# Attention beside a feed-forward gate on one core: the flags of the single-element waits taken one turn later, and the second score pair issued one row later

## The chip, the cores and the metric

The kernel runs on one core of a Trainium2 chip, in one launch. The metric is the device time of that launch in microseconds (us). Three runs of the kernel before took 1266.8, 1267.47 and 1267.58 us, a median of 1267.47.

## What is computed

```
xn = layernorm(x)                                   # x: 2048 x 512, float32
q, k, v = split(xn @ wqkv)                          # 32 heads of 16
p = softmax(q @ k^T * 16**-0.5)                     # 32 x 2048 x 2048
s = (p @ v) @ wo
h = relu(xn @ w1 + b1); g = silu((h * h) @ w2 + b2) # 512 -> 1792 -> 512
return x + s * g
```

## The kernel before

Everything is float32. Matrix products other than scores and values split their operands into a high and a low part (`fp32r`) and add three products; the scores do the same inside one contraction of 64 rows. The order of the instructions on each engine is written out by hand; nothing is scheduled afterwards, and semaphores are set from what each instruction reads and writes.

A first stage normalises x, makes q, k and v and writes q and k to memory. Then comes the main loop, 128 turns of four steps. A step `i` is one block of 128 keys against one block of 512 queries for a group of four heads, taken as two pairs `p` of two heads. Four turns finish one block of queries; the results of the values then leave `acc`.

The scores land in PSUM. Two buffers `S` of two banks alternate. `scores(i, p)` (L282) writes a whole pair into the next of them: two matmuls, one on the upper and one on the lower 64 rows of the array, side by side. `exps(i, p, src)` (L286) is ScalarE's exponential of a pair, into an SBUF tile `P`. Of the four steps of a turn one (`i + 3`) goes another way: `aside` (L300 to L305) computes one score at a time into the lone bank `single` (the profile's `lin`), VectorE copies it to `P` (L305), and the exponential works in place.

Between the scores TensorE works off the feed-forward products: `lin(...)` issues one half-array matmul of the current pair of blocks on the upper half, the lower, or both (L330; the bank pair is `spare`). `lin(0, 1)` is one row: two matmuls side by side. At the end of a turn come its values (L561, 32 matmuls into `acc`), then `finish`, which after every fourth turn copies `acc` out, on VectorE (L100) or, in turns with `turn_ends_first`, on ScalarE (L98).

`scores(i + 1, 0)` and `scores(i + 1, 1)` at the head of a turn reuse the buffers whose exponentials were the last two of the turn before. Between them stands `see` (L780 to L786), which touches single elements, so that an engine waits for another once and later instructions need no wait of their own for it:

- on ScalarE (L784), a copy of one element that the last exponential wrote, if `act_waits`;
- on VectorE (L786), the maximum of one element of the last exponential and one of the score buffer that it read, if `dve_waits`. As it reads that buffer, the next writer of the buffer, `scores(i + 1, 1)`, waits for it instead of ScalarE.

Where a flag is off, later instructions carry the wait themselves: the second pair waits for ScalarE directly, and the bank copy (L305) and the exponentials each get a second wait.

The flags are a list `alone` of two, computed in each turn `n`. Both are off in the turns of `tanh_in` (26, 28, 54, 56, 82, 84, 110, 112), in which ScalarE also does a tanh late in the turn. The first is off in turns with `turn_ends_first` (7, 15, 23 of each 28 up to 107). The second is off in every fourth turn (`n % 4 == 3`) without `turn_ends_first`. The second also decides about one more VectorE copy late in the same turn (L840).

```python
        alone = [n not in tanh_in and not turn_ends_first[0],
                 n not in tanh_in and (n % 4 < 3 or turn_ends_first[0])]
        if n:
            see(i, last[1], *alone)
```

Of the kernel before, what the change touches and what calls it, by code (L numbers as in the profile page):

```python
# [73 lines left out]
def fast_path(tc, sb, ps, env):  # L74
# [11 lines left out]
    def t(shape, dt, tag):  # L86

        cnt[0] += 1
        p = ps if tag in ("S", "lin", "acc") else sb
        if tag in BUFS:  # L90
            turn[tag] = turn.get(tag, -1) + 1
            n = turn[tag] % BUFS[tag]
            tag = f"{tag}{places[n] if tag == 'S' else n}"
        return p.tile(shape, dt, tag=tag, name=f"{tag}_{cnt[0]}")
# [183 lines left out]
    def score(i, p, hp, dst):  # L278
        qd, qc, kb = steps[i]
        k, q = ka[qd, kb // 8], qa[qd, qc]  # L280
        r = slice(64 * hp, 64 * hp + 64)
        mm(dst, k[r, p, 128 * (kb % 8):128 * (kb % 8) + 128], q[r, p], start=True, stop=True)  # L282

    def exps(i, p, src):
        if src is not None:
            act.activation(ptile[i, p], src, AF.Exp, scale=SCALE)  # L286

    def place(i, p):
        ptile[i, p] = t([128, 2, 512], FT, f"P{2 * ((i - 1) % 4) + p}")

    def scores(i, p):

        if i < len(steps):
            sc = t([128, 2, 512], FT, "S")
            place(i, p)
            for hp in range(2):
                score(i, p, hp, sc[:, hp])
            return sc

    def aside(i, p, hp):  # L300

        if hp == 0:
            place(i, p)
        score(i, p, hp, single)
        dve.tensor_copy(ptile[i, p][:, hp], single)  # L305
# [51 lines left out]
    def lin(*halves):  # L357
        if pair[0]:
            for half in halves:
                j = half ^ swapped[0]  # L360
                pair[0][j].issue(half, lin_banks[j])

    def lin_part(half, part):
        if pair[0]:
            j = half ^ swapped[0]
            pair[0][j].issue_part(half, lin_banks[j], part)

    def swap():
        if pair[0]:
            while any([pair[0][half ^ swapped[0]].issue(half, lin_banks[half ^ swapped[0]]) for half in range(2)]):  # L370
                pass
            swapped[0] ^= 1
            if not swapped[0]:
                pair[0][0].evict()
                pair[0] = None
# [21 lines left out]
    def split_piece(eng=None):  # L397
        if at_piece[1] == len(pieces):
            return
        j, layer, m = pieces[at_piece[1]]  # L400
        at_piece[1] += 1
        raw, q = raws.pop(0), PAIRS[m][1]
        wf[layer, m] = [t([128, 4, 256] if layer == 1 else [128, 2, 512], FR, f"wf{layer}{p}{q}") for p in "hl"]
        split(*wf[layer, m], raw, eng or dve, pool)
        load_piece()
# [149 lines left out]
    def values(i):  # L555
        qd, qc, kb = steps[i]
        if kb == 0:
            acc[0] = t([128, 512], FT, "acc")
        for j in (1, 2, 3, 0) if i % 2 else (0, 1, 2, 3):
            o = (4 * qd + j) * 17  # L560
            mm(acc[0][32 * j:32 * j + 32], vt[:, kb, o:o + 32], ptile[i, j // 2][:, j % 2],  # L561
               start=kb == 0, stop=kb == NK - 1)

    def finish(i):

        qd, qc, kb = steps[i]
        if kb < NK - 1:
            return
        if i == len(steps) - 1:
            return  # L570
        ou = t([128, 512], FT, "ou")
        cast(act if turn_ends_first[0] else dve, ou, acc[0])
        sp.dma_start(zdram[qd][qc], ou[16::32])
        for j in range(4):
            sp.dma_start(udram[qd // 2][qc][0, qd % 2, :, j], ou[32 * j:32 * j + 16])
        n = i // 4
        events.setdefault(2 * n + 2, []).insert(0, (load_sums, (qd, qc)))
        at(n + 2, rowsums, qd, qc)
# [24 lines left out]
    def gate_start(c, i):  # L603
        assert (c, i) in complete
        e = t([128, 2, 512], FT, "T")
        act.activation(e, y[c, i], AF.Tanh, scale=0.5)
        gated[c, i] = e
# [101 lines left out]
    tanh_in = {}  # L709
# [44 lines left out]
    def happen(time):  # L754
        for fn, a in events.pop(int(2 * time), ()):
            fn(*a)


    n = turn["S"]
# [7 lines left out]
    def rest(i, dst):  # L767

        group(dst, lambda p: onorm[2, 3][p][:, cut[i]], lambda p: wos[0][p][:, 3])

    def end_rest(i, src):

        o = t([128, 512], FT, f"wf2{'hl'[i // 2]}{i % 2}")
        dve.scalar_tensor_tensor(o, src, 0.5, gsb[2, i // 2][:, i % 2], op0=OP.mult, op1=OP.mult)
        pool.dma_start(out[1024 + 128 * i:1152 + 128 * i], o, accum_op=OP.add)

    turn_ends_first = [False]
    seen = t([1, 16], FT, "seen")

    def see(i, other, act_waits, dve_waits):  # L780

        last = ptile[i, 1][:1, 1, 511:]
        if act_waits:
            act.copy(seen[:, :1], last)  # L784
        if dve_waits:
            dve.tensor_tensor(seen[:, 8:9], last, other[:1, 0, :1], op=OP.max)  # L786

    for n in range(TURNS):
        i = 4 * n
        happen(n)  # L790
        make, end, split_now = fill[n]
        turn_ends_first[0] = n < LAST and end and not make and fill[n - 1][2] and n % per in (7, 15, 23)

        alone = [n not in tanh_in and not turn_ends_first[0],
                 n not in tanh_in and (n % 4 < 3 or turn_ends_first[0])]
        if make:
            pair[0] = make()
        pair0 = scores(i + 1, 0)
        if n:
            see(i, last[1], *alone)  # L800
        exps(i + 1, 0, pair0)
        aside(i + 3, 0, 0)
        lin(1)
        exps(i + 1, 1, scores(i + 1, 1))
        for _ in range(3):
            lin(0, 1)
        lin(0)
        if make and end:
            lin(1)
            lin(0)  # L810
            aside(i + 3, 0, 1)
        else:

            lin_part(1, 0)
            aside(i + 3, 0, 1)
            lin(0)
        exps(i + 2, 0, scores(i + 2, 0))
        if make and end:
            for j in range(2):
                pair[0][j].issue_whole(lin_banks[j])  # L820
            swap()
        else:
            lin_part(1, 1)
            lin(0, 1)
            lin(0, 1)
        exps(i + 2, 1, scores(i + 2, 1))
        aside(i + 3, 1, 0)
        lin(1)
        exps(i + 3, 0, ptile[i + 3, 0])
        if n in tanh_in:  # L830
            gate_start(*tanh_in[n])
        lin(0, 1)
        lin(0, 1)
        last = [scores(i + 4, 0)]
        lin(0, 1)
        lin(0, 1)
        lin(0)
        aside(i + 3, 1, 1)
        if alone[1]:
            dve.tensor_copy(seen[:, 8:9], single[:1, :1])  # L840
        exps(i + 3, 1, ptile[i + 3, 1])
        last.append(scores(i + 4, 1))
        for p in range(2):
            exps(i + 4, p, last[p])
        if n == TURNS - 1:
            two = t([128, 2, 512], FT, "S")
            rest(0, two[:, 0])
        swap()
        if n == LAST - 1:
            gsb.update({(2, i): y[2, i] for i in range(2)})  # L850
        if n == TURNS - 1:
            end_rest(0, two[:, 0])
        happen(n + 0.5)
        if split_now:
            split_piece()
        for j in range(4):
            values(i + j)
        finish(i + 3)
# [169 lines left out]
```

## Time and profile before

| what | value |
|---|---|
| median of three runs | 1267.47 us |
| the profiled execution, its own time | 1267.24 us |
| its span, first to last instruction | 1265.4 us |
| granted TensorE clock over the span | 0.998 |
| TensorE matmuls busy (PE) | 1246.9 us |
| ScalarE busy (ACT) | 1056.0 us |
| VectorE busy (DVE) | 693.3 us |
| single-element maximum on DVE (L786) | 99 times, 143 ns median |
| single-element copy on ACT (L784) | 107 times, 190 ns median |

The profile is that of one execution. A row of the timeline gives start and duration in us, engine, line, operation, output and inputs by the program's names, shapes and a count; a bracket at its end says how long the engine sat idle before and what ended that. PE's busy time is that of pipelined matmuls, whose ends are modelled. A group of two matmuls that run side by side on the halves of the array appears as one row with x2, and a row cut by the window that was asked for shows a smaller count.

### The profile page before, as it was taken

What the parts mean: (1) busy time and instruction counts of PE and PEld (TensorE: products, weight loads), DVE (VectorE), ACT (ScalarE), POOL (GpSimd) and SP (SyncE); (2) the same over time, 40 slices, a digit from 0 to 9 for tenths busy, and PEclk for the clock granted to TensorE, in tenths of its full rate; (3) what the DMA queues carried; (4) which work ended last, traced back from release to release, by engine and by line L of the source; (5) the groups of instructions that cost most, each with busy time, mean ns of one, the idle gap of its engine ahead of it and who ended that gap; (6) DMA issues with size and microseconds to landing.
All of it is one profiled execution on the core that took longest, in us unless ns stands there. A gap on an engine that the chain in (4) does not pass through costs nothing.

```text
span 1265.4 us, 24423 instructions
## 1 busy us (share of the span) xinstructions
PE 1246.9 (99%) x10029; PEld 715.3 (57%) x10029; DVE 693.3 (55%) x1263; ACT 1056.0 (83%) x1230; POOL 258.9 (20%) x150
## 2 busy tenths in 40 slices
PE   8999999999999999999999999999999999999997
PEld 7888755555555455555555555555555555554554
DVE  5542255555565664545465555555554646566655
ACT  4222599999999899999998999999999999998994
POOL 5000122122211221312022221120331212222112
PEclk9999999999999999999999999999999999999999
DMA  7565513231233232131423222333222132464445
GB/s 265 209 233 190 222 46 103 59 93 54 82 127 110 60 107 61 42 91 48 153 74 110 60 76 60 93 126 107 61 63 89 45 91 56 143 217 126 139 133 119
DMA packets 84937, 137.28 MB, mean 108 GB/s; under 512 B 26059, under 2 KB 40409, under 8 KB 83285
## 3 DMA queue, kind: packets, MB, share of 16 engines
q1 hardware_dynamic: 81668, 126.25, 31.4%
q0 software_dynamic: 2720, 8.65, 2.5%
q8 instruction: 79, 1.29, 0.4%
q10 hardware_dynamic: 432, 0.79, 0.2%
q14 instruction: 38, 0.30, 0.1%
HBM read 94.24 MB, written 41.41 MB: 107 GB/s over the span
## 4 chain that ended last, share of the span: by engine, by line
PE 91%; DVE 4%; issue 2%; ACT 1%; POOL 1%; DMA 0%; DVEq 0%; ACTq 0%
PE acc L561 32%; PE spare L330 25%; PE S L282 16%; PE S L111 9%; PE lin L282 6%; ACT P L286 1%; PE spare L350 1%; DVE T L413 1%; DVE P L305 1%; PE S L204 1%; DVE T L414 0%; DVE T L677 0%; PE spare L339 0%; POOL hl L104 0%; DVE ou L100 0%
## 5 line engine op out<-in xcount | busy, mean ns | idle before, releaser
L286 ACT ACTIVATE P<-S 128x1024 f32<-128x1024 f32 x768 | 735.7, 1018 | 55.4 <-PE S L282 54.4
L305 DVE COPY P<-lin 128x512 f32<-128x512 f32 x512 | 353.7, 691 | 363.2 <-PE lin L282 321.8
L561 PE MATMUL acc<-P,vt 128*32 128x512 f32 x4096 | 466.0, 595 | 0.0
L282 PE MATMUL S<-QA,KA 64*128 64x512 f32 x1536 | 340.0, 418 | 5.5 <-DVE seen L786 5.1
L286 ACT ACTIVATE P<-P 128x1024 f32<-128x1024 f32 x256 | 270.7, 1058 | 26.6 <-DVE P L305 16.8
L561 PEld LDWEIGHTS acc<-P,vt 128*32 128x32 f32 x4096 | 120.8, 109 | 266.0 <-issue 264.5
L282 PEld LDWEIGHTS S<-QA,KA 64*128 64x128 f32 x1536 | 152.7, 183 | 181.7 <-ACT P L286 123.3
L282 PE MATMUL lin<-QA,KA 64*128 64x512 f32 x512 | 206.1, 402 | 0.7 <-DVE P L305 0.5
L104 POOL TENSOR_TENSOR wf1l<-wr,wf1h 128x1024 fp32r<-128x1024 f32 x28 | 66.8, 2386 | 404.4 <-DVE wf1h L100 137.1
L104 POOL TENSOR_TENSOR hl<-T,hh 128x1024 fp32r<-128x1024 f32 x28 | 67.6, 2414 | 237.5 <-PE S L282 151.3
L104 POOL TENSOR_TENSOR wf2l<-wr,wf2h 128x1024 fp32r<-128x1024 f32 x28 | 66.7, 2382 | 206.2 <-PE acc L561 140.5
L282 PEld LDWEIGHTS lin<-QA,KA 64*128 64x128 f32 x512 | 94.2, 184 | 20.3 <-DVE P L305 6.3
L330 PE MATMUL spare<-xl,wf1h 64*128 64x512 f32 x440 | 105.5, 391 | 0.0
L330 PE MATMUL spare<-xh,wf1h 64*128 64x512 f32 x504 | 95.7, 390 | 0.0
L330 PE MATMUL spare<-xh,wf1l 64*128 64x512 f32 x504 | 95.6, 391 | 0.0
L330 PE MATMUL spare<-wf2l,hh 64*128 64x512 f32 x400 | 94.9, 391 | 0.0
L330 PE MATMUL spare<-wf2h,hh 64*128 64x512 f32 x448 | 85.7, 390 | 0.0
L330 PE MATMUL spare<-wf2h,hl 64*128 64x512 f32 x416 | 80.8, 390 | 0.0
L98 ACT CAST P<-S 128x512 fp32r<-128x512 f32 x30 | 17.7, 588 | 57.6 <-PE S L111 55.8
L330 PEld LDWEIGHTS spare<-xh,wf1h 64*128 64x128 f32 x504 | 59.8, 185 | 8.5
L330 PEld LDWEIGHTS spare<-xh,wf1l 64*128 64x128 f32 x504 | 60.1, 185 | 7.1
L330 PEld LDWEIGHTS spare<-xl,wf1h 64*128 64x128 f32 x440 | 60.0, 184 | 1.3
(213 smaller groups left out, 1150.5 us busy)
## 6 DMA issues: line engine op xcount, KB each, us to landing
wr<-in_B_w_dram SPq DMA_DIRECT2D x56, 512.0 KB
KA<-kd SPq DMA_DIRECT2D x64, 256.0 KB
QA<-qd SPq DMA_DIRECT2D x128, 128.0 KB
kd<-P SPq DMA_DIRECT2D x15, 512.0 KB
qd<-P SPq DMA_DIRECT2D x15, 512.0 KB
u<-ud SPq DMA_DIRECT2D x15, 512.0 KB
P<-in_A_x_dram SPq DMA_DIRECT2D x8, 512.0 KB
xd<-KA SPq DMA_DIRECT2D x4, 1024.0 KB
```

Of the source, the lines that this page charges most:

```text
L98: act.copy(dst, src)
L104: leng.tensor_tensor(lo, src, hi.bitcast(FT), op=OP.subtract)
L111: mm(dst, lhs(a, k), rhs(b, k), start=n == 0, stop=n == len(todo) - 1)
L204: nc.tensor.transpose(pt[:, k, 128 * j:128 * j + 128], xnorm[c, i][:, j, 128 * k:128 * k + 128], ident)
L282: mm(dst, k[r, p, 128 * (kb % 8):128 * (kb % 8) + 128], q[r, p], start=True, stop=True)
L286: act.activation(ptile[i, p], src, AF.Exp, scale=SCALE)
L305: dve.tensor_copy(ptile[i, p][:, hp], single)
L330: mm(bank, self.lhs(a, k)[r], self.rhs(b, k)[r], start=n == 0 and self.at[other] == 0, stop=n == len(self.todo[half]) - 1 and self.at[othe ...
L350: mm(bank[:, c], self.lhs(a, k)[r], self.rhs(b, k)[r, c], start=False, stop=False)
L413: dve.tensor_scalar(r[:, f], spare[:, f], b1t[:, 2 * m + f:2 * m + f + 1], 0.0, op0=OP.add, op1=OP.max)
L561: mm(acc[0][32 * j:32 * j + 32], vt[:, kb, o:o + 32], ptile[i, j // 2][:, j % 2], start=kb == 0, stop=kb == NK - 1)
```

## The change

`see` in turn `n` gets the flags that were computed in turn `n - 1`. In turn 1 they are those of turn 0. The flag of the late copy (L840) stays that of its own turn. Second, one of the three rows `lin(0, 1)` that stood behind the second score pair now stands ahead of it.

```diff
+    alone = []
     for n in range(TURNS):
...
-        alone = [n not in tanh_in and not turn_ends_first[0],
-                 n not in tanh_in and (n % 4 < 3 or turn_ends_first[0])]
+        alone, now = [n not in tanh_in and not turn_ends_first[0],
+                      n not in tanh_in and (n % 4 < 3 or turn_ends_first[0])], alone
         if make:
             pair[0] = make()
         pair0 = scores(i + 1, 0)
         if n:
-            see(i, last[1], *alone)
+            see(i, last[1], *now)
         exps(i + 1, 0, pair0)
         aside(i + 3, 0, 0)
         lin(1)
+        lin(0, 1)
         exps(i + 1, 1, scores(i + 1, 1))
-        for _ in range(3):
+        for _ in range(2):
             lin(0, 1)
         lin(0)
```

The built program has 100 maxima on VectorE instead of 99 and 107 copies on ScalarE as before. The maximum is left out in turns 4, 12, 20, 32, 40, 48, 60, 68, 76, 88, 96, 104, 116, 120, 124 and 29, 57, 85, 113, where it was, and is there in turns 3, 11, 19, 31, 39, 47, 59, 67, 75, 87, 95, 103, 115, 119, 123, 127 and 26, 54, 82, 110, where it was not. ScalarE's copy is left out in the turns behind `turn_ends_first` (8, 16, 24 and so on) and behind a tanh (27, 29 and so on), and is there in the turns themselves.

## The prediction

> **What bounds the kernel now.** I read the page's head and its chain first, then the main loop as one window, the waits, and at last single turns in the timeline.
>
> ```profile
> span 1265.4 us, 24423 instructions
> ...
> PE 1246.9 (99%) x10029; PEld 715.3 (57%) x10029; DVE 693.3 (55%) x1263; ACT 1056.0 (83%) x1230; POOL 258.9 (20%) x150
> ...
> PE 91%; DVE 4%; issue 2%; ACT 1%; POOL 1%; DMA 0%; DVEq 0%; ACTq 0%
> ```
> ```profile
> 155.10:1244.90 1089.80, 1083.82 (x9212) 584.47 (x9210) 616.15 (x1094) 1003.29 (x1145) 233.82 (x115) 1.00 0.30 92
> ```
> ```profile
> PEld S L282 <- DVE seen L786: 20.3, 46, 1.1
> ```
> The chain is TensorE almost throughout, and the window (127 turns, from the first values block to the last; its columns are us, busy time of PE, PEld, DVE, ACT, POOL, then clock and DMA) shows a clock of 1.00. So the matmul stream sets the time, and the change, which adds no matmul and drops none, can only move TensorE's stalls. The waits name one that fits: 46 times the weight load of a score pair sat until the single-element maximum at L786. Its 20.3 us overstate the loss, since a matmul was still running for part of each wait. How much is lost shows in the pitch of the turns: a turn is the time from one values block (`acc`, L561) to the next. I number turns from 0, as the loop does. First the head of turn 13, an undisturbed one:
>
> ```profile
> 258.52 0.64 PE L561 MATMUL acc<-P,vt 128*32 128x512 f32 x4
> ...
> 262.09 0.50 PE L282 MATMUL S<-QA,KA 64*128 64x512 f32 x2
> 262.43 0.39 PE L282 MATMUL lin<-QA,KA 64*128 64x512 f32 x1
> 262.63 1.03 ACT L286 ACTIVATE P<-S 128x1024 f32<-128x1024 f32 x1 [0.38 <-PE S L282]
> 262.67 0.39 PE L282 MATMUL S<-QA,KA 64*128 64x512 f32 x2
> 262.86 0.69 DVE L305 COPY P<-lin 128x512 f32<-128x512 f32 x1 [0.65 <-PE lin L282]
> 262.90 1.09 PE L330 MATMUL spare<-xh,wf1h 64*128 64x512 f32 x7
> 263.56 1.02 ACT L286 ACTIVATE P<-S 128x1024 f32<-128x1024 f32 x1
> ...
> 266.94 0.64 PE L561 MATMUL acc<-P,vt 128*32 128x512 f32 x4
> ```
> It takes 266.94 - 258.52 = 8.42 us. Two half-array matmuls run side by side, so a "row" costs the step from one start to the next: 262.90 - 262.67 = 0.23 us. The first score pair starts at 262.09 and the second at 262.67, 4.15 after the values block began. Turn 12 stands before it:
>
> ```profile
> 249.63 0.64 PE L561 MATMUL acc<-P,vt 128*32 128x512 f32 x4
> ...
> 253.35 0.69 DVE L100 COPY ou<-acc 128x512 f32<-128x512 f32 x1 [2.01 <-PE acc L561]
> 253.96 0.13 DVE L786 TENSOR_TENSOR seen<-P,S 1x1 f32<-1x1 f32 x1
> 254.15 0.50 PE L282 MATMUL S<-QA,KA 64*128 64x512 f32 x2 [0.20 <-DVE seen L786]
> ```
> Every fourth turn a result block ends, and DVE copies `acc` out. The maximum queues behind that copy and ends at 254.09. The second pair waits for it and starts at 254.15, 4.52 after the values block began and so 0.37 later than in turn 13; the turn takes 258.52 - 249.63 = 8.89 us, 0.47 more. That is the stall at issue.
>
> All 127 turns at 8.42 would be 1069.3 us; eight turns with a denser fill (4 and 5 of each 28) have more matmul time of their own, so the whole recoverable excess is below 1089.8 - 1069.3 = 20.5 us. That is a ceiling.
>
> **The change part by part.** From the two lists of flags as the code computes them, the maximum on DVE disappears in 19 turns (4, 12, 20, 29 and so on) and appears in 20 (3, 11, 19, 26 and so on). ACT's copy disappears in 20 and appears in 20. A single-element operation is 0.14 us on DVE and hides there; what matters is who waits.
>
> *A: 15 turns lose the maximum right behind DVE's `acc` copy* (4, 12, 20 of each 28, and 116, 120, 124). The second pair then waits for ACT's last exponential only, which was done before the pair started. What remains is shown by turn 28, which has DVE's `acc` copy and no maximum already now:
>
> ```profile
> 386.03 0.64 PE L561 MATMUL acc<-P,vt 128*32 128x512 f32 x4
> ...
> 389.75 0.69 DVE L100 COPY ou<-acc 128x512 f32<-128x512 f32 x1 [1.99 <-PE acc L561]
> 389.94 0.39 PE L282 MATMUL lin<-QA,KA 64*128 64x512 f32 x1
> ...
> 390.44 0.69 DVE L305 COPY P<-lin 128x512 f32<-128x512 f32 x1
> 391.22 0.46 PE L282 MATMUL lin<-QA,KA 64*128 64x512 f32 x1
> ...
> 394.52 0.64 PE L561 MATMUL acc<-P,vt 128*32 128x512 f32 x4
> ```
> It takes 394.52 - 386.03 = 8.49 us, 0.07 over the undisturbed turn: the copy of the lone score bank (L305) is late, and with it the next use of that bank. So a turn of kind A goes from 8.89 to 8.49: 0.40 saved, 15 x 0.40 = 6.0. The stall goes to the next `lin` matmul, which is late by those 0.07. At the end of the kernel DVE is later still:
>
> ```profile
> 1143.80 0.67 DVE L100 COPY ou<-acc 128x512 f32<-128x512 f32 x1
> 1144.45 0.67 DVE L305 COPY P<-lin 128x512 f32<-128x512 f32 x1
> 1144.58 0.50 PE L282 MATMUL S<-QA,KA 64*128 64x512 f32 x2 [0.60 <-DVE seen L786]
> 1145.72 0.40 PE L282 MATMUL lin<-QA,KA 64*128 64x512 f32 x1
> ```
> This is turn 116. Its bank copy can start when the `acc` copy ends, at 1144.47, and ends by 1145.16; in turn 28 `lin` followed such a copy by 391.22 - 391.13 = 0.09, so here it comes near 1145.25 where it now comes at 1145.72. That is 0.47; I keep 0.40. Bounds for A: 0.13 a turn (only the maximum's own duration, if the copy behind it was the real holder) and 0.47 (everything): 2.0 to 7.1.
>
> *B: 20 turns gain the maximum.* They lack it today and pay turn 28's 0.07; with it they look like turn 13. 20 x 0.07 = 1.4. Below, 0; above, the same 1.4.
>
> The bank copy starts 390.44 - 389.94 = 0.50 after `lin` in turn 28 and 262.86 - 262.43 = 0.43 in turn 13: the 0.07 again.
>
> By the Trainium skill (Perfetto Trace Analysis, section Identifying Dependency Chains) an instruction that waits for several engines may get separate semaphore instructions ahead of it; the bank copy without a maximum is such a one, and the trace agrees with its 0.07. By that rule alone A would cost 15 x 0.07 = 1.05 and not save 6.0, and the sum would give 1262.6. Turn 28 holds this cost already, so the sum stays with the rows.
>
> *C: turns behind a tanh on ACT lose both waits* (27, 29 and so on, 8 in all).
>
> ```profile
> 377.45 0.64 PE L561 MATMUL acc<-P,vt 128*32 128x512 f32 x4
> ...
> 398.69 0.14 DVE L786 TENSOR_TENSOR seen<-P,S 1x1 f32<-1x1 f32 x1 [0.24 <-ACT P L286]
> ...
> 403.27 0.64 PE L561 MATMUL acc<-P,vt 128*32 128x512 f32 x4
> ```
> Turn 27 takes 386.03 - 377.45 = 8.58, turn 29 takes 403.27 - 394.52 = 8.75. In turn 29 the maximum itself waits for ACT, and the second pair behind it for both; waiting for ACT alone, one row later, it has what it needs in time. Both fall to 8.49: 4 x 0.09 + 4 x 0.26 = 1.4. Bounds: 0 and 4 x 0.16 + 4 x 0.33 = 2.0, with no rest at all.
>
> *D: the row ahead of the second pair.* The same matmuls run in another order, so where nothing waits it costs nothing on TensorE, and where the second pair waits it covers 0.23 us. The cover of its cost on ACT: the second exponential starts at 263.56, behind the first; its scores now end at 262.67 + 0.39 = 263.06, and at 263.29 one row later. ACT follows its scores by 0.04 (262.59 to 262.63), so 263.56 - 263.33 = 0.23 us of margin are left. Turns that keep a late maximum gain the full row: turn 118, for one.
>
> ```profile
> 1157.35 0.64 PE L561 MATMUL acc<-P,vt 128*32 128x512 f32 x4
> ...
> 1161.57 0.13 DVE L786 TENSOR_TENSOR seen<-P,S 1x1 f32<-1x1 f32 x1
> ...
> 1166.15 0.64 PE L561 MATMUL acc<-P,vt 128*32 128x512 f32 x4
> ```
> 8.80 us, 0.38 lost, 0.23 of it covered; five such turns (108, 114, 118, 122, 126): 1.15. Five first-layer turns lose a little, as turn 14 does (next fence: 275.45 - 266.94 = 8.51): 5 x 0.08 = 0.4. Bounds: 0 and 5 x 0.38 + 0.4 = 2.3.
>
> *E: turns in which ACT makes the `acc` copy.* Twelve of them lose ACT's copy behind it, the twelve before get one.
>
> ```profile
> 215.75 0.64 PE L561 MATMUL acc<-P,vt 128*32 128x512 f32 x4
> ...
> 219.95 0.18 ACT L784 COPY seen<-P 1x1 f32<-1x1 f32 x1
> 220.04 1.01 ACT L286 ACTIVATE P<-S 128x1024 f32<-128x1024 f32 x1
> ...
> 224.30 0.64 PE L561 MATMUL acc<-P,vt 128*32 128x512 f32 x4
> ...
> 275.45 0.64 PE L561 MATMUL acc<-P,vt 128*32 128x512 f32 x4
> 283.91 0.64 PE L561 MATMUL acc<-P,vt 128*32 128x512 f32 x4
> ```
> Turn 8 takes 8.55, 0.13 over, with ACT late. Without its copy the exponentials start 220.04 - 219.95 = 0.09 earlier; I take 0.07 for 11 turns (108 is in D): 0.8. Turn 15, one of those before, takes 283.91 - 275.45 = 8.46 and should reach 8.42: 12 x 0.04 = 0.5. Bounds: 0 and 12 x 0.13 + 0.5 = 2.1.
>
> Sum: 6.0 + 1.4 + 1.4 + 1.55 + 1.3 = 11.65 us. The profiled execution took 1267.24 (its span 1265.4 and 1.8 around it), 0.23 below the median of 1267.47. 1267.24 - 11.65 = 1255.6; I name 1255.5.
>
> **The rivals.**
>
> *The stall only moves to the bank copy.* If in the 15 turns the copy at L305, behind DVE's queue, holds `lin` nearly as long, A yields 2.0: 11.65 - 4.0 = 7.65, time 1259.6. For it: turn 116's DVE rows touch each other. Against: turn 28 has the same queue and 8.49. Chance 0.11.
>
> *The lists do not fit the turns they are moved to.* Then the first edit nets nothing and only the row counts: 0.23 in the 15, in four of C and in five of D, and 0.4: 24 x 0.23 + 0.4 = 5.9, time 1261.3. For it: a missing maximum costs 0.07 wherever it is, and 39 turns change their flag. Against: the stall of turn 12 lies just where the flag of turn 11 would have dropped it. Chance 0.06.
>
> *ACT runs dry, and it is slower.* The place is the second exponential of each turn: if the row made it late, each later pair would be late by as much, since the pairs alternate between two buffers. With the whole row lost in 127 turns that is 29.2, less 11.65: 1284.8. It decides from 11.65 / 127 = 0.09 us a turn. For it: ACT is busy 1003.29 of 1089.80, 92%. Against: the 0.23 of margin. Chance 0.06.
>
> The Trainium skill (Trainium Kernel Development and Optimization, section Performance Expectations) calls matmul busy time a poor measure and trusts the share of weight loading. By it PE's 584.47 of 1089.80 leaves room and ACT would be the fuller engine, which is this rival's reading. The turns' pitch speaks against it.
>
> *Nothing measurable*, because a later transfer or the tail sets the end: 1267. The chain's DMA share of 0% speaks against it. Chance 0.03.
>
> **How the numbers follow.** The forecast has 0.74, with a range of its own of 1253 to 1258. The upper bounds together give 7.1 + 1.4 + 2.0 + 2.3 + 2.1 = 14.9, so 1252.3; the first rival closes the other end. The range 1252.3 to 1259.8 holds these two cases, some 0.83. Faster by over 0.2% (2.5 us, what can be told from no change) is the forecast and the first two rivals, 0.91; within it 0.03; slower 0.06.
>
> **What would show it.** Turn 12 at 8.49 and turn 3 at 8.42; the waits for the maximum ahead of `S` down from 46 to a handful; the second pair near 0.81 behind the first in undisturbed turns, and the second exponential still 0.93 behind the first. It is wrong if that distance grows, if `lin` waits for L305 by more than 0.1 in kind A, or if undisturbed turns leave 8.42.

## The result and the profile after

The changed kernel took 1253.98 us (median of 5 runs, 1253.39 to 1254.33) against 1267.47 (5 runs, 1266.8 to 1267.58): a ratio of 0.9894, with a 95% interval of 0.988 to 0.9909. It is 13.5 us faster where 12.0 were forecast. The profiled execution took 1253.39, with a span of 1251.6.

The page's line of busy times and its chain, and the two kinds of wait that end at a single-element operation or at an exponential ahead of a score pair:

```profile
PE 1239.9 (99%) x10029; PEld 719.6 (57%) x10029; DVE 695.8 (56%) x1264; ACT 1055.8 (84%) x1230; POOL 259.0 (21%) x150
...
PE 96%; DVE 2%; ACT 1%; POOL 1%; issue 0%; DMA 0%; DVEq 0%; ACTq 0%
```
```profile
PEld S L282 <- ACT P L286: 123.3, 225, 0.8
...
PEld S L282 <- DVE seen L786: 1.4, 4, 0.6
```
The waits for the maximum went from 46 (20.3 us) to 4 (1.4 us), with one maximum more in the program; those for ACT's exponentials stayed at 123.3 us (218 of them before, 225 now). DVE's share of the chain fell from 4% to 2%, TensorE's rose from 91% to 96%. The same work stands more densely. TensorE's busy time fell too, from 1246.9 to 1239.9 us for the same 10029 matmuls, so that this busy time holds part of the stalls and is not work alone.

The timeline of turn 12, in which DVE copies `acc` out, and of turn 13 behind it:

```profile
248.51 0.64 PE L561 MATMUL acc<-P,vt 128*32 128x512 f32 x4
...
252.08 0.51 PE L282 MATMUL S<-QA,KA 64*128 64x512 f32 x2
252.23 0.69 DVE L100 COPY ou<-acc 128x512 f32<-128x512 f32 x1 [1.99 <-PE acc L561]
252.42 0.39 PE L282 MATMUL lin<-QA,KA 64*128 64x512 f32 x1
252.88 0.40 PE L282 MATMUL S<-QA,KA 64*128 64x512 f32 x2
252.92 0.69 DVE L305 COPY P<-lin 128x512 f32<-128x512 f32 x1
253.70 0.46 PE L282 MATMUL lin<-QA,KA 64*128 64x512 f32 x1
...
256.99 0.64 PE L561 MATMUL acc<-P,vt 128*32 128x512 f32 x4
...
260.56 0.50 PE L282 MATMUL S<-QA,KA 64*128 64x512 f32 x2
261.10 1.03 ACT L286 ACTIVATE P<-S 128x1024 f32<-128x1024 f32 x1 [0.37 <-PE S L282]
261.36 0.39 PE L282 MATMUL S<-QA,KA 64*128 64x512 f32 x2
262.02 1.02 ACT L286 ACTIVATE P<-S 128x1024 f32<-128x1024 f32 x1
...
265.39 0.64 PE L561 MATMUL acc<-P,vt 128*32 128x512 f32 x4
```
Turn 12 takes 256.99 - 248.51 = 8.48 us instead of 8.89. Its second pair starts 0.80 behind the first, as in the undisturbed turn 13 (261.36 - 260.56): there is no stall left at it. The bank copy still starts 0.50 behind its `lin` (252.92 - 252.42), which is the 0.07 of turn 28 before. Turn 13 takes 8.40, and its second exponential starts 262.02 - 261.10 = 0.92 behind the first, where it was 0.93: ACT did not notice the row.

Summed from the starts of all 128 values blocks in both traces, the kinds of the prediction saved:

| kind | turns | forecast, us | measured, us |
|---|---|---|---|
| A, no maximum behind DVE's `acc` copy | 15 | 6.0 | 7.16 |
| B, a maximum gained | 20 | 1.4 | 1.53 |
| C, behind a tanh | 8 | 1.4 | 1.69 |
| D, the row alone | 10 | 1.55 | 1.45 |
| E, `acc` copy on ACT | 23 | 1.3 | 1.27 |
| all other turns | 51 | 0 | 0.15 |
| before the first and behind the last values block | | 0 | 0.51 |

Together 13.8, the difference of the spans.

### The profile page after: what moved, and what is told of

Same layout as the page of the kernel before. It is cut to its first block, busy times and chain, and to the rows that moved or that the text cites. A ratio compares the mean times of both kernels' runs of the same rounds, so it can differ in the third digit from the quotient of the medians.

```text
span 1251.6 us, 24417 instructions
## 1 busy us (share of the span) xinstructions
PE 1239.9 (99%) x10029; PEld 719.6 (57%) x10029; DVE 695.8 (56%) x1264; ACT 1055.8 (84%) x1230; POOL 259.0 (21%) x150
## 3 DMA queue, kind: packets, MB, share of 16 engines
q0 software_dynamic: 2720, 8.65, 2.4%
## 4 chain that ended last, share of the span: by engine, by line
PE 96%; DVE 2%; ACT 1%; POOL 1%; issue 0%; DMA 0%; DVEq 0%; ACTq 0%
PE acc L561 36%; PE spare L330 25%; PE S L282 16%; PE S L111 9%; PE lin L282 7%; PE spare L350 1%; PE S L204 1%; PE spare L339 0%; POOL hl L104 0%; DVE P L305 0%; DMA P<-in_A_x_dram 0%; PE acc L111 0%; ACT P L286 0%; DVE st L166 0%; ACT wf2h L98 0%
## 5 line engine op out<-in xcount | busy, mean ns | idle before, releaser
L305 DVE COPY P<-lin 128x512 f32<-128x512 f32 x512 | 354.0, 691 | 309.4 <-PE lin L282 265.4
L282 PE MATMUL S<-QA,KA 64*128 64x512 f32 x1536 | 335.8, 413 | 0.1
L282 PEld LDWEIGHTS S<-QA,KA 64*128 64x128 f32 x1536 | 154.1, 183 | 166.1 <-ACT P L286 123.3
L786 DVE TENSOR_TENSOR seen<-P,S 1x1 f32<-1x1 f32 x100 | 14.1, 141 | 116.5 <-ACT P L286 116.5
```

## The experiments

All ran beside the kernel before, in three groups on three chips; its medians there were 1267.38, 1267.85 and 1267.45 us. Savings by kind of turn are again sums over the starts of the values blocks, one profiled execution each.

**The flags alone.** The row goes back behind the second pair:

```diff
-        lin(0, 1)
         exps(i + 1, 1, scores(i + 1, 1))
-        for _ in range(2):
+        for _ in range(3):
             lin(0, 1)
```


> The flags one turn later, all three rows behind the second pair as before. My theory: the 15 turns behind an acc copy on DVE do not need the row, because the second pair then waits for ACT alone, so kind A stays at 8.48 to 8.49 us (turn 12). What is lost against the changed kernel is the row's own part: 1.1 in turns 108, 114, 118, 122, 126, 0.4 in the first-layer turns (turn 14 back at 8.50), and 0.1 to 0.2 in each turn behind a tanh, where ACT's last exponential ends too late for a second pair that stands a row earlier (turn 27 stays at 8.55 to 8.60). Sum about 2.5 to 3: 1256.5 to 1257. Rival that the flags net nothing and the row does the work: 1265 to 1267.

It took 1257.34 us (ratio 0.9921, 0.9904 to 0.9937), 10.0 below the kernel before. The rival that the flags net nothing is gone: kind A alone keeps 7.12 of its 7.16. The time lies a little above the 1256.5 to 1257 that were expected. Turn 12, and a turn behind a tanh, in this kernel's timeline:

```profile
248.72 0.64 PE L561 MATMUL acc<-P,vt 128*32 128x512 f32 x4
257.23 0.64 PE L561 MATMUL acc<-P,vt 128*32 128x512 f32 x4
...
375.47 0.64 PE L561 MATMUL acc<-P,vt 128*32 128x512 f32 x4
384.11 0.64 PE L561 MATMUL acc<-P,vt 128*32 128x512 f32 x4
```
Turn 12 takes 8.51, nearly as with the row (8.48). Turn 27 takes 8.64, where it took 8.58 in the kernel before and 8.48 with the row: there the row is what pays, and a little more than I had put down for this run (8.55 to 8.60). In turn 29 it is the flags first, from 8.75 to 8.54, and the row for the rest. All eight turns behind a tanh lose 1.03 against the changed kernel, kind D 1.50.

**The row alone.** The kernel before with

```diff
         lin(1)
+        lin(0, 1)
         exps(i + 1, 1, scores(i + 1, 1))
-        for _ in range(3):
+        for _ in range(2):
             lin(0, 1)
```


> The row ahead of the second pair, the flags as before. My theory: the row covers 0.23 us of each stall at the second pair: turn 12 goes from 8.89 to 8.66, turn 4 from 9.41 to 9.17, turn 14 to 8.42, turn 118 to 8.55; the turns without a maximum stay at 8.49 (turn 3). 5.9 to 6.6 us saved in all: 1260.8 to 1261.5. Rival that the row does all of it: 1254. Rival that the row hurts ACT: over 1267.

It took 1260.81 us (0.995, 0.9934 to 0.9967), 6.6 below the kernel before. Its turn 12:

```profile
249.27 0.64 PE L561 MATMUL acc<-P,vt 128*32 128x512 f32 x4
...
253.59 0.13 DVE L786 TENSOR_TENSOR seen<-P,S 1x1 f32<-1x1 f32 x1
253.78 0.50 PE L282 MATMUL S<-QA,KA 64*128 64x512 f32 x2
...
257.92 0.64 PE L561 MATMUL acc<-P,vt 128*32 128x512 f32 x4
```
The maximum is as late as before and holds the second pair as before, but one row was done meanwhile: 8.65, which is 8.89 - 0.24. The two edits alone save 10.0 + 6.6 = 16.6 and together 13.5. The 3.1 of overlap is the 15 turns of kind A, where either removes the same 0.23: summed by turns, the overlap there is 3.4, and within 0.2 of nothing in every other kind.

**No maximum at all.** The changed kernel without the operation at L786, a computation nobody reads:

```diff
-            see(i, last[1], *now)
+            see(i, last[1], now[0], False)
```


> The changed kernel without any of DVE's maxima at L786 (100 single-element operations less, nothing else; the output is unchanged). My theory: the maximum carries the bank copy's wait for ACT, so without it the copy at L305 starts 0.07 late in each turn that has one now, except where the lin matmul behind it comes later anyway (turns 4 and 5 of each 28) or another DVE operation has waited for ACT already: about 85 turns x 0.07 = 6 us, less 0.6 in turns 108, 118 and 122, which need no maximum: 1259 to 1260. Turn 13 goes from 8.41 to 8.48. Rival that the 0.07 belongs to the acc copy in every fourth turn and not to the missing maximum: 1253.4.

It took 1260.03 us, 6.0 more than the changed kernel. Its turn 13:

```profile
257.27 0.64 PE L561 MATMUL acc<-P,vt 128*32 128x512 f32 x4
...
261.18 0.39 PE L282 MATMUL lin<-QA,KA 64*128 64x512 f32 x1
...
261.67 0.69 DVE L305 COPY P<-lin 128x512 f32<-128x512 f32 x1 [1.81 <-PE lin L282]
262.45 0.46 PE L282 MATMUL lin<-QA,KA 64*128 64x512 f32 x1
...
265.74 0.64 PE L561 MATMUL acc<-P,vt 128*32 128x512 f32 x4
```
DVE had nothing else to do for 1.81 us, and still its copy starts 0.49 behind `lin` and not 0.43, and the turn takes 8.47. So the 0.07 belongs to the missing maximum and not to the `acc` copy. An operation of 0.14 us that nobody reads saves 0.07 of TensorE's time in some 80 turns, because it takes a wait off the copy that TensorE needs next. In turns 4 and 5 of each 28, whose `lin` comes later anyway, taking it away cost nothing, as expected. The Trainium skill (Perfetto Trace Analysis, section Identifying Dependency Chains) names the extra semaphore instruction for a second engine; the trace agrees, at 0.07 us here. The trace counts the separate semaphore instructions at the bank copy's line (L305), first in the changed kernel, then without the maxima:

```profile
L305 DVEq EVENT_SEMAPHORE  x54: 21/21/49, 150.4 to 1204.2; - x54
...
L305 DVEq EVENT_SEMAPHORE  x254: 21/21/50, 150.1 to 1235.4; - x127
```
In turn 13 without the maximum this instruction starts at 261.6, when `lin`'s matmul is done, and the copy 0.06 behind it. That is the lost time. Two turns (38 and 112) lost 0.3 to 0.4 each in this profile with DVE idle; why, the trace does not show, and their 0.8 is part of the 6.0.

**Every wait in every turn.**

```diff
-            see(i, last[1], *now)
+            see(i, last[1], True, True)
```


> The changed kernel with both waits in every turn from 1 on (19 + 8 maxima and 20 ACT copies more). My theory: the maxima behind DVE's acc copy hold the second pair again, now with a row's cover: turn 12 at 8.65, turn 4 at 9.15, turn 116 at 9.05; ACT's copy behind its acc copy puts turn 8 back to 8.53. About 5 to 6 us lost: 1259 to 1260. Rival that the order of the flags does not matter once the row is there: 1254.

It took 1259.84 us, 5.9 more than the changed kernel. Turn 12 in its timeline:

```profile
248.80 0.64 PE L561 MATMUL acc<-P,vt 128*32 128x512 f32 x4
257.46 0.64 PE L561 MATMUL acc<-P,vt 128*32 128x512 f32 x4
```
8.66, as with the row alone. By turns the loss is 5.6: 4.4 where a maximum now stands behind DVE's `acc` copy (kind A and turns 28, 56, 84 and 112), 0.6 behind a tanh, where both waits are new, and 0.6 in kind E, where ACT's copy (L784) is. With the run before it, both ends are shown: both waits in every turn cost 5.9, no maximum anywhere 6.0, and the list in the right turns is worth that much either way.

**More rows ahead of the second pair.** Two of the three, then all three:

```diff
         lin(1)
-        lin(0, 1)
+        for _ in range(2):
+            lin(0, 1)
         exps(i + 1, 1, scores(i + 1, 1))
-        for _ in range(2):
-            lin(0, 1)
+        lin(0, 1)
```


> The changed kernel with two rows instead of one ahead of the second pair. In the changed kernel's trace the second exponential starts 0.267 us behind the end of its scores and needs 0.04, so 0.227 are left of the margin; the second row takes 0.232. My theory: undisturbed turns stay at 8.41 to 8.43, the second exponential is late by 0.00 to 0.02, and only turns 108, 118 and 122 gain (0.4 in all): 1253 to 1255, no difference that can be told. Rival that ACT is already short with one row: 0.23 a turn, 1280.

> Three rows ahead of the second pair. My theory: the margin is used up, the second exponential starts 0.23 late, and the fourth pair, which waits for the buffer that it reads and has 0.01 us to spare now (172 ns from exponential to pair, 162 being needed), is late by 0.2: some 118 turns x 0.2 to 0.23 = 24 to 27 us, 1278 to 1281; turn 13 at 8.62 to 8.65. Rival that ACT's 8% of idle time absorbs it: 1254.

Two rows took 1253.68 us, three took 1277.65 (1.0077, 1.006 to 1.0094), just under the 1278 to 1281 that were expected. Turn 13 with two rows:

```profile
256.71 0.64 PE L561 MATMUL acc<-P,vt 128*32 128x512 f32 x4
...
260.82 1.02 ACT L286 ACTIVATE P<-S 128x1024 f32<-128x1024 f32 x1 [0.38 <-PE S L282]
261.76 1.03 ACT L286 ACTIVATE P<-S 128x1024 f32<-128x1024 f32 x1
...
265.14 0.64 PE L561 MATMUL acc<-P,vt 128*32 128x512 f32 x4
```
And with three:

```profile
258.91 0.64 PE L561 MATMUL acc<-P,vt 128*32 128x512 f32 x4
...
263.03 1.03 ACT L286 ACTIVATE P<-S 128x1024 f32<-128x1024 f32 x1 [0.39 <-PE S L282]
263.75 0.39 PE L282 MATMUL S<-QA,KA 64*128 64x512 f32 x2
264.18 1.03 ACT L286 ACTIVATE P<-S 128x1024 f32<-128x1024 f32 x1
265.26 0.50 PE L282 MATMUL S<-QA,KA 64*128 64x512 f32 x2
...
267.56 0.64 PE L561 MATMUL acc<-P,vt 128*32 128x512 f32 x4
```
The step from the first exponential to the second is 0.92 with one row, 0.94 with two and 1.15 with three; the turns take 8.40, 8.43 and 8.65. With three rows the second pair ends after the first exponential does (264.14 against 264.06), ACT waits, and the fourth pair (265.26), which needs the buffer that the second exponential reads, waits for ACT. Its row starts 0.05 behind the end of that exponential (265.21); the 162 ns of the expectation are my estimate, fitted to the turns, which no row shows. Over the 127 turns it is 23.7 us more than with one row. So the slower rival had the right place and, at 0.23 in an undisturbed turn, the right price; what decided against it was that a margin of 0.23 us, one row wide, was left behind the first row. The second row uses it up, the third costs its whole length.

**The last `acc` copies on ACT.** In turns 115, 119 and 123 of the changed kernel:

```diff
-        turn_ends_first[0] = n < LAST and end and ...
+        turn_ends_first[0] = n in (115, 119, 123) or n < LAST and end and ...
```


> The changed kernel with the acc copy of turns 115, 119 and 123 on ACT instead of DVE (and the flags that go with it). My theory: in turns 116, 120 and 124 of the changed kernel the bank copy behind DVE's acc copy holds lin; with the copy on ACT they go from 8.71, 8.64 and 8.82 to 8.50, like turn 8: 0.65 us, too little to tell by the time, but not by the turns. 1253.3. Rival that the stall there comes from elsewhere: the three turns stay.

It took 1253.67 us. Turn 116, first as the changed kernel has it:

```profile
1128.79 0.64 PE L561 MATMUL acc<-P,vt 128*32 128x512 f32 x4
...
1132.70 0.39 PE L282 MATMUL lin<-QA,KA 64*128 64x512 f32 x1
1132.84 0.67 DVE L100 COPY ou<-acc 128x512 f32<-128x512 f32 x1
...
1133.44 0.67 DVE L305 COPY P<-lin 128x512 f32<-128x512 f32 x1
...
1134.16 0.50 PE L282 MATMUL lin<-QA,KA 64*128 64x512 f32 x1
...
1137.50 0.64 PE L561 MATMUL acc<-P,vt 128*32 128x512 f32 x4
```
and with the copy on ACT:

```profile
1128.65 0.64 PE L561 MATMUL acc<-P,vt 128*32 128x512 f32 x4
1137.13 0.64 PE L561 MATMUL acc<-P,vt 128*32 128x512 f32 x4
```
8.71 became 8.48; turns 120 and 124 went from 8.64 and 8.82 to 8.50 and 8.56. In these three turns of kind A the stall had moved to the bank copy, as the first rival had it: the copy starts 1133.44 - 1132.70 = 0.74 behind its `lin`. The median is 0.3 below the changed kernel's, which can't be told from nothing; the turns show it.

**Together.** Two rows, the last `acc` copies on ACT, and no maximum in turn 108, beside the changed kernel itself on the same chip:

> The three things the turns point to, together: two rows ahead of the second pair, the acc copies of turns 115, 119 and 123 on ACT, and no maximum in turn 108. From the turns of the runs so far: 0.54 in turns 108 to 126 for the second row, 0.58 in turns 116, 120 and 124, and 0.15 more in turn 108, which should come to 8.49. 1.2 to 1.3 us below the changed kernel of the same call, 0.1%. Rival that the second row takes back in the undisturbed turns what it gives, since the margin on ACT is used up to the last 0.01: no difference.

> The changed kernel itself once more, on the chip of the run before it, so that the two can be set side by side: 1253.4 to 1254.3.

They took 1252.42 us (4 runs, 1252.26 to 1253.19) and 1254.34 (4 runs, 1254.04 to 1254.88). The runs of the two do not overlap: 1.9 us, 0.15%. The turns account for 1.28 of it, 0.60 in turns 108 to 126 of kind D and 0.68 in kind A, nearly all of that in turns 116, 120 and 124, as expected (1.2 to 1.3); the rest lies within the spread of the runs.

## Why the prediction was right

That TensorE's order sets the time, and that the change can only move its stalls, held: the undisturbed turns stayed at 8.40 to 8.44, and 13.1 of the 13.8 us came from turns that the prediction had named. The sum had been 11.65, so 2.1 were missing: 1.16 in A, 0.3 in C, 0.5 outside the turns, where executions of these kernels differ by as much, and little in the rest.

*A* had the right mechanism and the wrong size; its 7.16 lies even above the 7.1 that I had called everything. I took turn 12's 0.40 for all 15. The eight turns like it did save 0.41. But turns 4, 32, 60 and 88 saved 0.57 on average, more than the 0.47 that I had allowed, for they had lost more (9.41 in turn 4, with 8.81 to reach): their bank copy is late too, but their next `lin` stands later in the order. The timeline of turn 4 after:

```profile
180.28 0.64 PE L561 MATMUL acc<-P,vt 128*32 128x512 f32 x4
...
184.74 0.68 DVE L305 COPY P<-lin 128x512 f32<-128x512 f32 x1
...
185.58 0.39 PE L282 MATMUL lin<-QA,KA 64*128 64x512 f32 x1
...
189.09 0.64 PE L561 MATMUL acc<-P,vt 128*32 128x512 f32 x4
```
The copy ends at 185.42, `lin` follows by 0.16 without a stall, and the turn takes 8.81, like turn 5, whose kind it is. At the kernel's end the three turns saved 0.52 on average, and yet my own sign against the forecast came true there: in turn 116 the weight load of `lin` waits 0.34 for the bank copy, where more than 0.1 was to mean that it is wrong. I had let the bank copy start when the `acc` copy ends; it starts 0.07 earlier (1133.44 against 1132.84 + 0.67), and `lin` came 0.2 sooner than I had put it.

*B* was right at 0.07 a turn (0.08 measured), shown by taking the maxima away.

*C* came to 8.46 to 8.48, not 8.49, and for another reason than I gave; that the two figures lie so close is luck. Turn 29 after:

```profile
392.03 0.64 PE L561 MATMUL acc<-P,vt 128*32 128x512 f32 x4
...
395.94 0.39 PE L282 MATMUL lin<-QA,KA 64*128 64x512 f32 x1
...
396.37 0.69 DVE L305 COPY P<-lin 128x512 f32<-128x512 f32 x1 [0.46 <-PE lin L282]
...
400.50 0.64 PE L561 MATMUL acc<-P,vt 128*32 128x512 f32 x4
```
The copy starts 0.43 behind `lin` with no maximum ahead of it. Another operation of DVE in that turn (L612, at 393.38) reads what the tanh wrote and has waited 0.74 for ACT already. The copy's separate semaphore instruction, next in the queue at 393.6, is through 2.8 us before the copy and costs nothing. That L612 carries the wait fits both rows; no run takes it away. The remaining 0.05 arises behind the fourth pair, whose weight load waits 0.20 for ACT's exponential there and not at all in turn 13; that ACT is late because of the tanh is argued, not tried.

*D* was right: the row is worth about the 0.23 where the maximum stays late (turn 118 from 8.80 to 8.54, turn 108 from 9.07 to 8.85; 1.06 in the five turns against 1.15) and nothing where nothing waits.

*E* had the right mechanism: turn 8 came to 8.49, turn 15 to 8.42. The halves were 0.6 and 0.7 where 0.8 and 0.5 were forecast, so that the sum agrees to 0.03 is luck.

Of the rivals, the stall that only moves was true in part of three turns and not of 15; the flags that net nothing were refuted by the flags alone; ACT running dry was refuted for one row and shown for three; that nothing can be measured is gone with the 13.5 us.

## What to carry to other kernels

Where one engine sets the time, read the pitch of each turn and compare turns that differ in one thing; a turn that lacks an operation already gives the price of dropping it elsewhere. A tiny operation that only collects a wait pays if its engine is idle there and costs if the engine is late, so it belongs in a list of turns, and such a list has to be checked against the turn in which it acts. Ahead of a wait, put work as wide as the margin of the engine fed by it, and measure that margin first: here it was one row and a bare second one, and the third cost 24 us.

## What was not expected of the hardware

A wait taken off an instruction is worth time even when it has long been met: DVE's copy, with DVE idle for 1.81 us ahead of it, started 0.49 us behind its `lin` with two waits and 0.43 with one. It is not the idleness: without the maxima, turn 8's copy came 0.50 behind after 0.46 of idle time, and in turn 29 of the changed kernel 0.43 behind after the same 0.46. Nor does every second wait cost: it did where the separate semaphore instruction came right ahead of the copy, and did not where, as in turn 29, it was through long before. And operations of one engine overlap at their ends: in turn 116 the bank copy's row starts 0.07 us before the end of the `acc` copy's.
